# Two-column size sums, a deeper fold of layer 1 scores and staged operand sums in a two-layer attention and SwiGLU kernel

## The chip, the cores and the metric

The kernel runs on one core of one Trainium2 chip. Its time is the device time of one execution in microseconds. A figure for a kernel is the median of several executions; where two kernels are compared, both ran in the same rounds on the same chip.

## The reference, cut to what matters

```python
# x: 1 x 2048 x 1024; all inputs bf16; the same weights in both layers
def A(x, wqkv, wo):      # attention, 32 heads of 32; each position sees 8 keys, 2 apart, backwards
    ...                  # q, k, v = x @ wqkv; softmax over the 8 scores; sum of values; @ wo
def B(x, w1, w3, w2):    # F = 3584
    return (silu(x @ w1) * (x @ w3)) @ w2

for layer in range(2):
    x = x + A(layernorm(x), wqkv, wo)
    x = x + B(layernorm(x), w1, w3, w2)
```

## The kernel before

The positions are cut into four chunks of 512. Eight stages (layer, chunk) of B follow one another on TensorE (PE), with the attention of later chunks woven in. The first two stages of B multiply plainly. While they run, ScalarE and VectorE make scaled fp16 sums and differences of weight blocks and store them; the other six stages use a scheme with seven products of half-size blocks instead of eight, which needs those weights and four sums of the activations.

**The order of instructions on each engine is decided when the program is built, by a model of time inside the kernel.** Every helper adds a modelled cost to a modelled clock, and `background` gives VectorE a waiting piece of work only if it is modelled to fit before the next piece that PE needs. On the chip each engine then goes through its list in that order: the two traces of the kernel after show the same order of all 2126 instructions on VectorE, 1388 on ScalarE and 308 on GpSimd.

```python
def pe(n, ready=0.0):
    now["pe"] = max(now["pe"], ready) + n * MM            # MM = 0.216
    return now["pe"] + 0.1
def dve(cost, ready=0.0):
    now["dve"] = max(now["dve"], ready) + cost
    ...
def dma(kb, ready=0.0, issue=0.45):                       # modelled landing of a load
    now["sp"] = max(now["sp"], ready, now["dma"] - 9.0) + issue
    now["dma"] = max(now["dma"], now["sp"] + 0.2) + kb / 380
    return now["dma"] + 1.3
def background(until):
    while True:
        best = None
        for queue in (norms, makes, adds, values, scores):
            step = head(queue)                            # (cost, ready, emit)
            if step is not None:
                start = max(now["dve"] + 0.3, step[1])
                if start - 0.3 + step[0] <= until and (best is None or start < best[0]):
                    best = start, queue
        if best is None:
            return
        take(best[1])
```

The parts that the change touches (cut):

```python
def norm_sums(key):                       # four sums of activations for a stage of B
    while not sums_free[0]:
        yield "blocked"                   # until the stage before has left all three buffers
    ...
    yield step(s1, a21, a22, ALU.add)         # each: cost 0.62, ready when xnT is modelled to land
    yield step(s2, s1, a11, ALU.subtract)
    yield step(a21, a11, a21, ALU.subtract)
    yield step(s4, a12, s2, ALU.subtract)

def weight_size(m, g, w, at, got):        # squares of a weight group, summed over partitions
    ...
    for i in range(2):
        nc.tensor.matmul(ps[:], lhsT=ones[:], rhs=size[:, m, g, i:i + 1], start=i == 0, stop=i == 1)
    makes.append([scale_item(ps, pe(2, t)), None])

def differences(m, g, a, r):              # VectorE, for stored weight blocks
    for out, x, y in ((4, 5, 1), (1, 1, 0), (2, 5, 1), (6, 3, 2)):
        yield 0.46, r, lambda: nc.vector.tensor_tensor(b[:, out], b[:, x], b[:, y], op=ALU.subtract)

def score_steps():                        # per half chunk
    ...
    yield 0.0, ready + 2.0, lambda: None  # modelled landing of kT, plus 2 us
    yield from tree(W, tree_bufs[0], mul_qk, lambda w_: psm[:, w_], True)   # leaves two partials
    ...
    for i in range(2):                    # gather: sums over a head's dimensions, on PE
        for a in range(4):
            nc.tensor.matmul(L[32 * a:32 * (a + 1), :, :], lhsT=gather[:],
                             rhs=psm[:, :, i, a * BLK:(a + 1) * BLK], start=i == 0, stop=i == 1, ...)
    at["t"] = pe(3, t) + 0.2

def b_stage(u, hold):
    ...
    if u >= TU:
        force(adds, lambda: ("B", l, c) in sums_of)       # all four sums before the first product
```

In the profile these are named by what they write: `L` is the gather, `psm` a partial of the scores, `st` the gate and up products of the fast scheme, `w` the down product, `ps` a projection to q, k or v, `po` the output projection, `xnT` the transposed normed input, and `big` a buffer that holds, among others, weight differences and operand sums.

## Time and profile before

| | before |
|---|---|
| median, lowest to highest (three executions; the result below has a fourth) | 1545.78 us, 1545.72 to 1547.3 |
| PE busy, of a span of 1546.5 us | 1529.9 us (99%) |
| VectorE (DVE) busy | 1191.9 us (77%) |
| PE's waits, all together | 12.5 us |

The profiled execution itself took 1548.26 us, longer than the timed ones. The first lines of the page of the kernel before (PEld is TensorE's loading of weights, ACT is ScalarE, POOL is GpSimd; SPq, further down, is SyncE, which issues loads and stores):

```profile
span 1546.5 us, 25176 instructions
PE 1529.9 (99%) x9694; PEld 992.7 (64%) x9694; DVE 1191.9 (77%) x2048; ACT 883.3 (57%) x1388; POOL 158.8 (10%) x308
```

PE is the bound. A busy PE need not be an efficient one, so the starts of matmuls were looked at as well: they follow each other at 215 to 216 ns with 512 columns and 109 ns with 256 nearly everywhere. What is to be won is PE's own work and its few waits. From the list of what PE waited for (engine, line, tile, releaser: us in total, times, longest):

```profile
PE L L595 <- DVE psm L506: 4.1, 1, 4.1
PE w L1057 <- DVE hT L1028: 2.6, 3, 1.4
PE w L1057 <- ACT big L1077: 1.9, 4, 0.6
```

The largest wait is a single one, and the timeline shows its making (start us, length us, engine, line, operation, in brackets the idle time just before and what ended it):

```profile
522.88 8.33 SPq L831 DMA_DIRECT2D qkv_d<-hT  x2
531.30 8.73 SPq L263 DMA_TRANSPOSE xnT<-xn  x2
...
542.21 0.69 DVE L287 TENSOR_TENSOR big<-xnT 128x1024 f16<-128x1024 f16 x1 [10.08 <-DMA xnT<-xn]
...
545.68 0.42 DVE L506 TENSOR_TENSOR psm<-tree 128x512 bf16<-128x512 bf16 x1
546.16 1.05 PE L595 MATMUL L<-psm,gather 128*32 128x512 bf16 x8 [4.06 <-DVE psm L506]
...
554.49 1.22 DVE L582 TENSOR_TENSOR tree<-qT,kT 128x2048 bf16<-128x2048 bf16 x1 [1.46 <-DMA kT<-qkv_d]
```

SyncE issues two transposed loads only after two stores, which wait for PE's pace. VectorE stands 10 us at the first operand sum (L287), for those loads; the last folds of `psm` stand behind it in the list, though their inputs are there; PE's gather waits for the folds. The Trainium skill ("TensorE: Matmul & The Clock Gate", specification table, engine queue depth) calls VectorE's queue strict FIFO, and this is what it looks like.

The stall has a second cost. The windows view (start and end, length, busy time of the engines, granted PE clock, DMA share, GB/s) shows the clock of the stretch:

```profile
541.00:560.00 19.00, 14.94 (x63) 7.97 (x61) 12.94 (x19) 5.39 (x8) 2.19 (x4) 0.82 1.01 317
```

Eleven matmuls after the stall start 427 ns apart instead of 216, 2.3 us more. The skill (same page, Part 1) says that an idle window of about 3.4 us halves the clock; here an idle of 4.1 us did.

The groups whose counts the change alters or whose cost it moves (line, engine, operation, tiles, shapes, count, then busy us and mean ns of one, then idle before):

```profile
L595 PE MATMUL L<-psm,gather 128*32 128x512 bf16 x128 | 10.3, 399 | 4.1 <-DVE psm L506 4.1
L872 PE MATMUL size<-size,ones 128*128 128x1 f32 x56 | 7.0, 229 | 0.0
```

These durations overlap. What a burst delays PE is read from starts instead: the time from the start of the matmul before it to the start of the one after it, less that matmul's usual 216 or 109 ns. A size burst (two fp32 matmuls, each in two records) costs 0.363 us, with starts 28, 112, 112 and 111 ns apart. In the same way a wait comes out some 0.2 us longer from the starts than the idle time that the views list; where the text gives a longer figure than the view, it is from the starts. A gather burst of eight costs 0.641 us: four start 2 to 5 ns apart, 216 ns later the next four. The skill ("TensorE: Matmul & The Clock Gate", Part 3) gives about 4 ns between matmuls in separate column tiles; the trace agrees.

### The profile page before, as it was taken

What the parts mean: (1) busy time and instruction counts of PE and PEld (TensorE: products, weight loads), DVE (VectorE), ACT (ScalarE), POOL (GpSimd) and SP (SyncE); (2) the same over time, 40 slices, a digit from 0 to 9 for tenths busy, and PEclk for the clock granted to TensorE, in tenths of its full rate; (3) what the DMA queues carried; (4) which work ended last, traced back from release to release, by engine and by line L of the source; (5) the groups of instructions that cost most, each with busy time, mean ns of one, the idle gap of its engine ahead of it and who ended that gap; (6) DMA issues with size and microseconds to landing.
All of it is one profiled execution on the core that took longest, in us unless ns stands there. A gap on an engine that the chain in (4) does not pass through costs nothing.

```text
span 1546.5 us, 25176 instructions
## 1 busy us (share of the span) xinstructions
PE 1529.9 (99%) x9694; PEld 992.7 (64%) x9694; DVE 1191.9 (77%) x2048; ACT 883.3 (57%) x1388; POOL 158.8 (10%) x308
## 2 busy tenths in 40 slices
PE   9999999999999989999999999999999999999999
PEld 7666644444444568675685766866677667686866
DVE  4788988889889688989798958798668977435345
ACT  4885466657565346555574564756557446554633
POOL 1210102111111000101001020100101001000000
PEclk9999999999999999999999999999999999999999
DMA  9777969798898798979979888797979988878885
GB/s 330 202 222 203 265 222 319 255 305 284 249 329 290 241 307 316 316 265 295 296 269 339 309 261 284 277 318 275 334 249 316 339 296 276 303 275 327 311 292 207
DMA packets 261432, 439.57 MB, mean 284 GB/s; under 512 B 73856, under 2 KB 201088, under 8 KB 245056
## 3 DMA queue, kind: packets, MB, share of 16 engines
q1 hardware_dynamic: 248464, 390.90, 76.6%
q0 software_dynamic: 12704, 46.93, 8.2%
q8 instruction: 76, 1.25, 0.3%
q14 instruction: 44, 0.36, 0.1%
q10 hardware_dynamic: 144, 0.13, 0.0%
HBM read 345.90 MB, written 67.90 MB: 268 GB/s over the span
## 4 chain that ended last, share of the span: by engine, by line
PE 83%; DVE 9%; ACT 3%; DMA 3%; issue 1%; POOL 1%; SPq 1%; ACTq 0%; DVEq 0%; POOLq 0%
PE st L1122 28%; PE ps L820 18%; PE w L1057 11%; PE po L762 7%; PE pg L1243 6%; PE acc L1274 6%; PE pu L1252 6%; DVE tree L656 1%; DMA wqkv<-in_A_wqkv_dram 1%; DVE tree L502 1%; PE pq L436 1%; DVE tree L582 1%; DVE hT L1028 1%; DMA xnT<-xn 1%; DVE hT L1140 1%
## 5 line engine op out<-in xcount | busy, mean ns | idle before, releaser
L820 PE MATMUL ps<-xnT,wqkv 128*128 128x512 f16 (+1 forms) x1472 | 323.3, 381 | 0.3 <-DMA wqkv<-in_A_wqkv_dram 0.2
L1122 PEld LDWEIGHTS <-early 128*128 128x128 f16 x2688 | 262.8, 98 | 38.2 <-issue 1.4
L820 PEld LDWEIGHTS <-wqkv 128*128 128x128 bf16 x1472 | 210.7, 144 | 111.8 <-issue 5.8
L1057 PE MATMUL w<-t,hT 128*128 128x512 f16 x1008 | 226.4, 379 | 4.6 <-DVE hT L1028 2.6
L1122 PEld LDWEIGHTS <-late 128*128 128x128 f16 x2016 | 197.0, 98 | 31.2 <-issue 3.2
L582 DVE TENSOR_TENSOR tree<-qT,kT 128x2048 bf16<-128x2048 bf16 x128 | 156.3, 1221 | 30.0 <-ACT big L824 14.8
L502 DVE TENSOR_TENSOR tree<-tree 128x1024 bf16<-128x1024 bf16 x256 | 175.1, 684 | 0.9
L1122 PE MATMUL st<-xnT,late 128*128 128x256 f16 x1344 | 174.2, 273 | 1.0 <-DVE big L1178 0.7
L1057 PEld LDWEIGHTS <-hT 128*128 128x128 f16 x1008 | 98.0, 98 | 118.5 <-DVE hT L1028 5.4
L1122 PE MATMUL st<-big,early 128*128 128x256 f16 x1344 | 172.2, 273 | 0.2
L1122 PE MATMUL st<-xnT,early 128*128 128x256 f16 x1344 | 165.7, 273 | 0.0
L656 DVE TENSOR_TENSOR tree<-At,vT 128x2048 bf16<-128x2048 bf16 x128 | 156.2, 1220 | 7.9 <-DMA At<-E 6.5
L1151 ACT COPY st<-st 128x512 f32<-128x512 f32 x84 | 48.4, 576 | 125.1 <-PE st L1122 124.3
L762 PE MATMUL po<-wo,oT 128*128 128x512 bf16 x512 | 115.9, 379 | 0.9 <-DVE x_sb L767 0.9
L1252 PE MATMUL pu<-xnT,w3t 128*128 128x512 f16 x448 | 105.8, 379 | 0.0
L1243 PE MATMUL pg<-xnT,w1t 128*128 128x512 f16 x448 | 105.8, 379 | 0.0
L824 ACT CAST hT<-ps 128x512 bf16<-128x512 f32 x96 | 55.6, 585 | 81.5 <-PE ps L820 80.3
L1163 DVE TENSOR_TENSOR st<-st,big 128x512 f32<-128x512 f32 x84 | 58.4, 695 | 51.9 <-ACT big L1160 51.8
L1274 PE MATMUL acc<-w2t,hT 128*128 128x512 bf16 x448 | 98.2, 379 | 0.0
L1131 ACT ACTIVATE sg<-st,down_scale 128x512 bf16<-128x512 f32 x126 | 86.5, 687 | 11.5 <-PE st L1122 10.9
L1122 PE MATMUL st<-big,late 128*128 128x256 f16 x672 | 87.1, 273 | 0.0
L762 PEld LDWEIGHTS <-oT 128*128 128x128 bf16 x512 | 50.1, 98 | 56.8 <-issue 1.2
(166 smaller groups left out, 1912.0 us busy)
## 6 DMA issues: line engine op xcount, KB each, us to landing
early<-t_d SPq DMA_DIRECT2D x84, 1024.0 KB, 6.5
late<-t_d SPq DMA_DIRECT2D x84, 768.0 KB, 6.4
t<-t_d SPq DMA_DIRECT2D x42, 1024.0 KB, 7.1
t<-t_d SPq DMA_DIRECT2D x42, 768.0 KB, 5.3
wqkv<-in_A_wqkv_dram SPq DMA_DIRECT2D x28, 1024.0 KB, 8.2
w1t<-in_B_w_dram SPq DMA_DIRECT2D x14, 1024.0 KB, 9.3
w3t<-in_B_w_dram SPq DMA_DIRECT2D x14, 1024.0 KB, 11.5
t_d<-big POOLq DMA_DIRECT2D x28, 512.0 KB, 7.1
```

Of the source, the lines that this page charges most:

```text
L502: nc.vector.tensor_tensor(b, b, buf[:, 4:8, :], op=ALU.add)
L582: V.tensor_tensor(pr, qT[:], kT[:, :, k0:k0 + TCH], op=ALU.mult)
L656: V.tensor_tensor(tm.rearrange("p w (a e) -> p w a e", a=4), At[:].rearrange("p a w e -> p w a e"), win, op=ALU.mult)
L762: nc.tensor.matmul(ps[:], lhsT=oT[:, t, j * P:(j + 1) * P], rhs=wo[:, t, hh * 512:(hh + 1) * 512], start=(t == 0), stop=(t == KT - 1))
L820: nc.tensor.matmul(ps[:], lhsT=ws[kk // KH][:, kk % KH, t::KT], rhs=xnT[:, kk, :], start=(kk == 0), stop=(kk == KT - 1))
L1057: nc.tensor.matmul(out[:], lhsT=lhs[:, k, j * P:(j + 1) * P], rhs=w[:, k, :], start=start and k == 0, stop=k == nq - 1, skip_group_check=True)
L1122: nc.tensor.matmul(out[:, a, :], lhsT=w[:, a, blk, k, :], rhs=rhs[:, k, :], start=start and a == 0 and k == 0, stop=k == KQ - 1, skip_grou ...
L1131: nc.scalar.activation(sg[:], src, ACTF.Silu, scale=inv)
L1163: nc.vector.tensor_tensor(G["D"][:], G["D"][:], su, op=ALU.add)
L1243: nc.tensor.matmul(pg[:], lhsT=w1t[:, kk, fi * P:(fi + 1) * P], rhs=xnT[:, kk, :], start=(kk == 0), stop=(kk == KT - 1))
L1252: nc.tensor.matmul(pu[:], lhsT=w3t[:, kk, fi * P:(fi + 1) * P], rhs=xnT[:, kk, :], start=(kk == 0), stop=(kk == KT - 1))
L1274: nc.tensor.matmul(acc[:], lhsT=hT[:, f, j * P:(j + 1) * P], rhs=tiles[hh][f // nq][:, f % nq, :], start=(f == 0), stop=(f == f1 - f0 - 1))
```

## The change

Its intent: take small matmuls off PE, hand scales and operand sums out as early as their inputs and buffers allow, and make VectorE's weight differences less serial. The diff also adds three functions that would use the fast scheme for the v projection (`size_of_v`, `sums_of_v`, `v_products`), and moves the product pipeline into a function of its own for them. They are never called. The core, cut:

```diff
 def norm_sums(key):
-    while not sums_free[0]:
-        yield "blocked"
-    sums_free[0] = False
     ...
-    yield step(s1, a21, a22, ALU.add)
-    yield step(s2, s1, a11, ALU.subtract)
-    yield step(a21, a11, a21, ALU.subtract)
-    yield step(s4, a12, s2, ALU.subtract)
+    for name, i, out, x, y, op in (("P5", 0, s1, a21, a22, ALU.add), ("P6", 1, s2, s1, a11, ALU.subtract),
+                                   ("P3", 2, s4, a12, s2, ALU.subtract), ("P7", 3, a21, a11, a21, ALU.subtract)):
+        while (sums_free[i] is None) if i < 3 else key in plain_left:
+            yield "blocked"
+        ...
+        yield 0.61, ready, lambda: nc.vector.tensor_tensor(out, x, y, op=op)
+        sums_at[key, name] = now["dve"] + 0.1
     # a buffer is free after the last product that reads it; run() forces only the sum it needs
@@ score_steps
-    yield from tree(W, tree_bufs[0], mul_qk, lambda w_: psm[:, w_], True)
+    parts_ = 2 if l == 0 else 1
+    yield from tree(W, tree_bufs[0], mul_qk, lambda w_: psm[:, w_, 0:parts_], l == 0)
     ...
-        for i in range(2):
+        for i in range(parts_):
-        at["t"] = pe(3, t) + 0.2
+        at["t"] = pe(1.5 * parts_, t) + 0.2
@@ weight_size
-                scale_of(ps[:], up, down)
+                nc.vector.tensor_reduce(down, ps[:], op=ALU.add, axis=AX.X)
+                scale_of(down, up, down)
-            for i in range(2):
-                nc.tensor.matmul(ps[:], lhsT=ones[:], rhs=size[:, m, g, i:i + 1], start=i == 0, stop=i == 1)
-            makes.append([scale_item(ps, pe(2, t)), None])
+            nc.tensor.matmul(ps[:], lhsT=ones[:], rhs=size[:, m, g, :], start=True, stop=True)
+            makes.insert(0, [scale_item(ps, pe(1, t)), None])
@@ differences (and the same for the down weights)
-        for out, x, y in ((4, 5, 1), (1, 1, 0), (2, 5, 1), (6, 3, 2)):
-            yield 0.46, r, lambda: nc.vector.tensor_tensor(b[:, out], b[:, x], b[:, y], op=ALU.subtract)
+        for out, x, y in ((4, 5, 1), (1, 1, 0), (2, 4, 0), (6, 3, 2)):
+            yield 0.40, r, lambda: nc.vector.tensor_tensor(
+                b[:, out], b[:, x], b[:, y], op=ALU.add if (x, y) == (4, 0) else ALU.subtract)
@@ not shown: side_tile() takes open scales before it hands out a side buffer; a scale's modelled cost goes from 0.8 to 1.0; the unused v functions
```

## The prediction

> **What bounds the kernel now.** TensorE. The page shows PE busy 99% of 1546.5 us at a granted clock of 0.997; VectorE 77%, ScalarE 57%. Matmuls start one after another at 216 ns (512 columns) and 109 ns (256) nearly everywhere. The list of waits gives PE only 12.5 us in all. The largest, 4.1 us, is at 546.2: the head-gathering matmul of scores (L) waits for VectorE's psm. The timeline shows why: VectorE stands 10.1 us at 542.2 at the first operand sum, for a transposed load of xnT that was queued behind two stores on SyncE. After it eleven matmuls take about 427 instead of 216 ns (granted clock 0.82 in 541 to 560, windows view), so the place costs some 6.5 us. The Trainium skill ("TensorE: Matmul & The Clock Gate", Part 1) says that an idle window of about 3.4 us halves the clock; the trace agrees. Other PE waits: 2.6 us for hT sums and 1.9 us for copies in the down product, 0.9 us each for the rest.
>
> **What the change does.** The three new functions for V (sizes, sums, products) are never called: 0 us.
> 1. Size of a weight group: four fp32 passes x14 become two. A burst now delays PE by 0.363 us; its starts are 28, 112, 112, 111 ns apart, so about 0.22 us goes: 14 x 0.22 = 3.1 us of PE. VectorE gains a tiny reduce (0.17 us, as the existing one) x14 = 2.4 us. Scales go to the front of their queue.
> 2. Layer 1 scores: a gather burst goes from 8 to 4 matmuls; it costs 0.641 us, its second half 0.216 us: 8 x 0.216 = 1.7 us of PE. VectorE gets 64 more folds like oT<-tree, 0.285 us each: 18 us over layer 1, where it is busy 601 of 723 us (windows).
> 3. Differences: the third no longer reads the second's result; some 0.06 to 0.1 us x42, 3 to 4 us of VectorE.
> 4. Operand sums staged per buffer, forced only before the product that needs them: PE waits for them today only through the stall at 546, and there the transposes are late, not the buffers. Nothing directly.
>
> **On the critical path.** 1 and 2 come off PE, the bound: -4.8 us. 3, 4 and the added folds are off it, but shift the kernel's modelled clocks, which decide the order of instructions; small waits may go or appear. Whether the stall stays depends on whether the transposes are issued before or after a store; I give 40% that it goes (-2.6 us in the mean), and +1 to 2 us for new waits on a busier VectorE. Together about 1540 us, 0.4% faster; 8 in 10 between 1533 and 1547.
>
> Chances: faster by over 2% 0.01, within 2% 0.97, slower by over 2% 0.02.
>
> **What would show it.** Size matmuls 56 to 28, bursts delaying PE 0.14 us; gather matmuls 128 to 96, layer 1 bursts 0.43 us; folds of 128x256 from 128 to 192; VectorE busy up by 10 to 16 us, PE busy down by 5; PE's waits with or without the 4.1 us on psm, and that stretch's clock.
>
> **What would make it wrong.** A reordering that puts VectorE behind a late load elsewhere (4 us plus a cold clock each); the added folds delaying the sums before the down product; scales forced early stalling VectorE; the stall moving rather than going.

## The result

| | before | after |
|---|---|---|
| first measurement, median (lowest to highest) | 1546.04 us (1545.72 to 1547.3) | 1544.22 us (1543.84 to 1544.88) |
| ratio, 95% interval | | 0.9987 (0.997 to 1.0004) |
| second measurement, five rounds, median | 1547.29 us | 1543.54 us |
| ratio, 95% interval | | 0.9975 (0.9963 to 0.9988) |
| span of the profiled execution | 1546.5 us | 1542.1 us |

A ratio is the mean time of one kernel's runs over that of the other's of the same rounds, so it is not quite the ratio of the medians. With five rounds the gain is clear of noise, at 2 to 6 us. The two traces differ by 4.4 us, more than the medians do (1.8 and 3.8 us): the trace of the kernel before is of an execution that was slower than its timed ones.

The page of the kernel after:

```profile
span 1542.1 us, 25098 instructions
PE 1521.5 (99%) x9595; PEld 990.2 (64%) x9634; DVE 1200.9 (78%) x2126; ACT 884.8 (57%) x1388; POOL 156.8 (10%) x308
```

The counts show that some matmul records are missing: 9634 weight loads, but 9595 matmuls. So "PE busy" is not to be compared to the microsecond here, and the starts of matmuls that both traces have are used. The altered groups, after:

```profile
L609 PE MATMUL L<-psm,gather 128*32 128x512 bf16 x96 | 8.1, 386 | 0.9 <-DVE psm L519 0.9
L897 PE MATMUL size<-size,ones 128*128 128x2 f32 x28 | 3.9, 209 | 0.0
...
L519 DVE TENSOR_TENSOR psm<-tree 128x256 bf16<-128x256 bf16 x64 | 18.3, 285 | 0.3
```

Size records went from 56 to 28 and a burst from 0.363 to 0.140 us. Layer 1 has four gathers in a burst, which costs 0.426 us instead of 0.641. VectorE has the 64 new folds, 18.3 us when their durations are added; its busy time rose by 9.0 us, a little less than the 10 to 16 of the prediction. PE's waits are another list than before, and together they went from 12.5 to 14.5 us:

```profile
PE st L1086 <- DVE st L1110: 3.8, 1, 3.8
PE ps L841 <- ACT hT L845: 1.8, 1, 1.8
PE po L776 <- DVE x_sb L781: 1.6, 2, 0.8
PE st L1086 <- DVE big L303: 1.4, 1, 1.4
...
PE ps L841 <- DMA wqkv<-in_A_wqkv_dram: 1.2, 2, 1.0
PE L L609 <- DVE psm L519: 0.9, 1, 0.9
```

The wait of 4.1 us on `psm` is gone; one of 3.8 us on a sum of `st` has come, and others in the projection `ps`, in `po` and, at 941 us, for an operand sum (`big`). The waits of `w` for `hT` (2.6 us) are gone too. The timeline of the stretch in which the stall stood:

```profile
526.91 4.48 PE L841 MATMUL ps<-xnT,wqkv 128*128 128x512 f16 x20 [1.81 <-ACT hT L845]
...
528.99 0.68 DVE L303 TENSOR_TENSOR big<-xnT 128x1024 f16<-128x1024 f16 x1
...
532.36 11.45 PE L841 MATMUL ps<-xnT,wqkv 128*128 128x512 f16 x52 [0.97 <-DMA wqkv<-in_A_wqkv_dram]
...
554.50 1.23 DVE L595 TENSOR_TENSOR tree<-qT,kT 128x2048 bf16<-128x2048 bf16 x1 [4.29 <-DMA kT<-qkv_d]
...
568.61 0.68 DVE L515 TENSOR_TENSOR tree<-tree 128x1024 bf16<-128x1024 bf16 x1
569.22 0.69 DVE L1110 TENSOR_TENSOR st<-st,big 128x512 f32<-128x512 f32 x1
...
569.96 1.87 PE L1086 MATMUL st<-big,late 128*128 128x256 f16 x8 [3.80 <-DVE st L1110]
```

The operand sum now finds its loads landed (no idle before 528.99), so PE reaches the stage of `st` sooner: at 559.9 instead of 566.8. But `kT` is used from 554.5 on, as before to the hundredth. VectorE has the folds of those scores, and products of values, in its list ahead of the sum of `st` (L1110) that PE needs, so PE waits for it. The stall did not go; it moved by 24 us. The clock follows it (windows view, after):

```profile
541.00:560.00 19.00, 19.00 (x96) 12.15 (x94) 9.10 (x12) 7.53 (x12) 2.20 (x4) 1.00 1.04 339
...
570.00:574.00 4.00, 4.00 (x25) 3.08 (x25) 4.00 (x7) 2.33 (x4) 0.00 (x0) 0.65 0.43 177
```

How the lead of the kernel after grows and shrinks is best seen from the starts of the same matmul (counted within its kind) in both traces:

```
start before   start after   difference   what lies since the row above
   192.0          192.6         +0.6      start of the program, loads
   487.5          484.0         -3.5      14 shorter size bursts; a wait of 1.1 us for po at 216 gone
   537.6          537.6          0.0      new waits of PE at 515, 532 (for loads) and 527 (for ScalarE)
   557.8          550.8         -6.9      the stall on psm and its cold clock gone
   577.8          576.2         -1.6      the new stall at 570 and its cold clock
   924.0          923.9         -0.1      new waits of 0.9 to 1.1 us at 612, 756 and 759; shorter gathers
  1126.6         1123.7         -2.9      waits of w for hT gone, shorter gathers; a new wait of 1.6 us at 941
  1267.1         1263.3         -3.8      one wait of 0.8 us of w gone, shorter gathers
  1546.5         1542.1         -4.4      a second wait of 0.8 us of w gone
```

### The profile page after: what moved, and what is told of

The parts are those of the page before. It is cut to its first block, busy times and chain, and to the rows that moved or that the text cites. A ratio compares the mean times of both kernels' runs of the same rounds, so it can differ in the third digit from the quotient of the medians. Undisturbed runs are those within 1.5% of the kernel's fastest.

```text
span 1542.1 us, 25098 instructions
## 1 busy us (share of the span) xinstructions
PE 1521.5 (99%) x9595; PEld 990.2 (64%) x9634; DVE 1200.9 (78%) x2126; ACT 884.8 (57%) x1388; POOL 156.8 (10%) x308
## 4 chain that ended last, share of the span: by engine, by line
PE 55%; DVE 4%; DMA 3%; ACT 3%; issue 1%; POOL 1%; ACTq 0%; DVEq 0%; POOLq 0%
PE st L1086 29%; PE w L1235 15%; PE ps L841 6%; PE po L776 4%; DMA qkv_d<-hT 1%; DMA t_d<-big 1%; DMA kT<-qkv_d 1%; DVE tree L595 1%; DMA xnT<-xn 1%; DVE tree L515 1%; ACT sg L1297 0%; DVE tree L670 0%; ACT big L1043 0%; ACT xn L323 0%; ACT L1297 0%
## 5 line engine op out<-in xcount | busy, mean ns | idle before, releaser
L776 PE MATMUL po<-wo,oT 128*128 128x512 bf16 x487 | 111.6, 379 | 2.9 <-DVE x_sb L781 1.6
L1110 DVE TENSOR_TENSOR st<-st,big 128x512 f32<-128x512 f32 x84 | 58.4, 695 | 50.2 <-ACT big L1107 50.1
```

What stands on the lines that cost most here:

```text
L776: nc.tensor.matmul(ps[:], lhsT=oT[:, t, j * P:(j + 1) * P], rhs=wo[:, t, hh * 512:(hh + 1) * 512], start=(t == 0), stop=(t == KT - 1))
L1110: nc.vector.tensor_tensor(G["D"][:], G["D"][:], su, op=ALU.add)
```

## The experiments

Twelve kernels were run, each with five rounds against the kernel before, and all gave a correct result. The theory with which they started was A: PE's saved work is saved time, and the rest is the order that the model makes of it. Its rivals are in the expectations.

### The size part alone

```diff
 # the kernel before, with the reduce and the two-column matmul of the change; still append, pe(2, t), cost 0.8
```

The order of all other instructions was compared with that of the kernel before and is the same; only the 14 reduces are new on VectorE.

> The kernel before with the two-column size matmul and the small reduce alone; the modelled costs are left as they were, so that every other instruction stands where it stood. Theory A (PE work saved is time saved): 14 bursts lose 0.22 us each, so about 3.1 us faster, ratio 0.998; the 4.1 us stall on psm near 543 stays, as does its cold clock. Theory B (what the change saved was never on the critical path, the 1.8 us came from a different order): within 0.5 us of the kernel before.

Measured: 1545.17 us against 1547.29, ratio 0.9987 (0.9975 to 1.0). In the traces the size bursts lose 3.1 us in all, each visible as a step of 0.22 us, and the end comes 2.2 us sooner; waits that are 0.4 to 0.8 us longer than before, among them one for a wqkv load at 1085 us, take the rest. The stall stays (3.9 us at 545). Theory A holds for this part, at two thirds of its size.

### The fold alone, in the old order

```diff
 # the kernel before; layer 1: four gathers, and after each psm of two partials one more add
+    V.tensor_tensor(psm[:, w_, 0:1], psm[:, w_, 0:1], psm[:, w_, 1:2], op=ALU.add)
 # no modelled cost for it, and the gather still counted as pe(3, t)
```

> The kernel before with the extra fold of layer 1 scores and the halved gather alone, modelled costs kept, so the order is that of before with 64 folds put in. Theory A: 8 bursts lose 0.216 us each, 1.7 us faster, ratio 0.9989, and VectorE's 18 us more cost nothing. Theory C (the folds are paid for by PE in layer 1): waits of the down product for VectorE's sums grow from 2.6 us and the kernel is as fast as before or up to 3 us slower.

Measured: 1549.03 us against 1547.29, ratio 1.0012 (0.9999 to 1.0024): slower, if anything. Eight steps of 0.22 us are there in the starts, and more is lost between 880 and 1090 us. PE's waits in 850 to 1110 us were 2.6, 0.7, 0.4 and 0.2 us before; with the fold they are

```profile
PE w L1065 <- DVE hT L1036: 2.6, 3, 1.5
PE st L1130 <- ACT st L1159: 0.9, 1, 0.9
...
```

and six more lines of 0.3 to 0.7 us. Theory C is the right one here, in another shape than it was put: the wait for `hT` did not grow, new ones came. VectorE's 18 us were not free.

### Both parts, in the old order

> Both parts in the order of the kernel before. Theory A: the savings add, 4.8 us faster, about 1541.2 us, which is faster than the whole change (1544.2); then the order of the whole change costs some 3 us. Theory B or C: no faster than the whole change.

Measured: 1547.74 us against 1547.29, ratio 1.0007 (0.9994 to 1.0021); the trace ends 1.1 us sooner than that of before. The parts do not bring 4.8 us: the fold eats what the size part gives.

### The whole change, again

> The whole change once more on the same chip as the three parts, for a narrow interval: 1.8 us faster than before if the medians so far hold, 4.4 us if the two traces do. Theory A with a dearer order: slower than the two parts alone by 2 to 4 us.

Measured: 1543.54 us, ratio 0.9975 (0.9963 to 0.9988). So the whole is better than its two PE savings in the old order, against what theory A expected: the new order does not cost 3 us, it is worth some.

### The fold as the change writes it

```diff
 # the kernel before, with the tree and the gather of the change, their costs in the model
-            yield from tree(W, tree_bufs[0], mul_qk, lambda w_: psm[:, w_], True)
+            parts_ = 2 if l == 0 else 1
+            yield from tree(W, tree_bufs[0], mul_qk, lambda w_: psm[:, w_, 0:parts_], l == 0)
```

> The kernel before with the fold of layer 1 scores as the change writes it: the folds and the shorter gather stand in the kernel's own model of time, so the order may move. Theory D (the 1.7 us that the fold cost in the old order came from VectorE running later than its model says, at three places between 985 and 1090 us): with the folds in the model the gathers' 1.7 us are kept, ratio 0.998 to 0.999. Rival (VectorE is simply too busy there and the fold costs whatever the model knows): ratio 1.001 as in the fold alone.

Measured: 1544.59 us against 1547.38, ratio 0.9981 (0.9968 to 0.9993). The same folds and gathers as in the fold alone: there about 1.7 us slower than before, here 2.8 us faster. Of PE's waits in 850 to 1110 us there are left:

```profile
PE st L1123 <- ACT big L1161: 2.2, 1, 2.2
PE w L1058 <- ACT big L1078: 0.5, 1, 0.5
```

The waits of `w` for `hT` are gone. That the folds are in the model is the only difference in the text of the two programs that matters; what it did is another order (some 200 of 2112 VectorE instructions stand elsewhere than in the kernel before), and how much of the 4.5 us is foresight and how much luck, this pair cannot tell.

### The size part with that fold

```diff
 # the kernel before with the fold as in the kernel above, and the size part as in the first experiment; nothing else
```

Apart from the size sums and their reduces, all engines have the order of the kernel above.

> The kernel before with the size part and the fold as the change writes it, nothing else: no staging, no new differences, no new queue places. If the parts add: 2.1 + 2.8 = 4.9 us faster, ratio 0.9968, a little faster than the whole change (0.9975 in its round). If they don't: like the fold alone, 0.998.

Measured: 1541.99 us (1541.46 to 1543.66) against 1546.93, ratio 0.9969 (0.9955 to 0.9983), and a trace of 1540.0 us. In this order the parts add: 2.1 us for the size part and 2.8 for the fold, measured apart, make 4.9, and 4.9 is what both bring. Two of the change's parts are thus worth about as much as the whole (0.9975, 0.9963 to 0.9988; the intervals overlap), although the old stall is still there:

```profile
PE L L596 <- DVE psm L506: 3.9, 1, 3.9
```

### The whole change without its fold

> The whole change without its fold (layer 1 keeps two partials and eight gathers). Theory D: slower than the whole change by about 1.7 us (ratio to before 0.9985 against 0.9975). Rival: faster than the whole change by 1 to 2 us (0.9965). The late part has another order either way, so up to 1.5 us of it may be that.

Measured: 1543.53 us against 1547.38, ratio 0.9971 (0.9958 to 0.9983), and a trace 0.1 us shorter than that of the whole change. Theory D, which had it slower, is not met. The rival's 0.9965 lies inside the interval, but the two traces are of one length: within the change, the fold is worth nothing that can be measured. What it takes off PE, 1.7 us, comes back as waits in the late part; the trace without it has no wait of PE at 941 us and none before the gather at 756 (1.6 and 1.1 us with it), and from 578 to 1538 us it gains 1.5 us on the whole change.

### The whole change without staging

```diff
-            while (sums_free[i] is None) if i < 3 else key in plain_left:
-                yield "blocked"
+        while not all_free[0]:
+            yield "blocked"          # and: order P5, P6, P7, P3; all forced at the start of the stage
```

> The whole change with the operand sums as before (all four at once when all three buffers are free, forced at the start of the stage). The two programs differ in the order of 29 of 2128 VectorE instructions. My reading (PE never waits for a buffer of sums): within 0.5 us of the whole change, ratio 0.9975. Rival (staging is what the change is for): slower by 2 us or more, with new PE waits at the start of the stages.

Measured: 1545.47 us against 1547.38, ratio 0.999 (0.9976 to 1.0004), where the whole change had 0.9975 in its rounds. The intervals overlap, so the traces decide. Without staging PE waits at 1262.9 and at 1405.4 us, 0.8 us each, as in the kernel before at 1266.0 and 1408.5; with it these waits are gone. In the kernel before, the four sums for the next stage stand in one piece in front of a sum that the down product needs:

```profile
1262.06 0.68 DVE L287 TENSOR_TENSOR big<-xnT 128x1024 f16<-128x1024 f16 x1
...
1263.99 0.68 DVE L287 TENSOR_TENSOR big<-xnT,big 128x1024 f16<-128x1024 f16 x1
1264.60 0.69 DVE L1080 TENSOR_TENSOR w<-w,big 128x512 f32<-128x512 f32 x1
1265.38 0.59 ACT L1077 COPY big<-w 128x512 f32<-128x512 f32 x1 [1.95 <-DVE w L1080]
...
1266.01 3.18 PE L1057 MATMUL w<-t,hT 128*128 128x512 f16 x14 [0.62 <-ACT big L1077]
```

In the kernel after they are spread over the products before, as each buffer comes free:

```profile
1244.79 0.68 DVE L303 TENSOR_TENSOR big<-xnT 128x1024 f16<-128x1024 f16 x1
...
1252.71 0.69 DVE L303 TENSOR_TENSOR xnT<-xnT 128x1024 f16<-128x1024 f16 x1
...
1258.19 9.12 PE L1235 MATMUL w<-t,hT 128*128 128x512 f16 x41
...
1260.77 0.69 DVE L1258 TENSOR_TENSOR w<-w,big 128x512 f32<-128x512 f32 x1
```

Staging pays, then, at the two places where one fast stage follows another directly: between the starts of the same matmuls the traces with and without it part there by 0.7 and by 0.6 us, 1.3 us together. It does so not because PE waited for a sum, but because four sums in a row made something else late. The trace without staging also has a wait of 1.9 us near 302 us, of `po` on `x_sb`, at a place where the two programs have the same instructions in the same order; in the second trace of the whole change it is 0.5 us long in the starts. It is variation between runs, and it is made up, mostly because the stall at 570 is here followed by no cold clock; at 1200 us the two traces are level.

### The size part, operand sums later

```diff
 # the size part alone, and for the stage whose loads came late:
-            return 0.62, xnT_at[key], lambda: ...
+            return 0.62, xnT_at[key] + (9.0 if key == ("B", 0, 2) else 0.0), lambda: ...
```

> The size part alone, with the operand sums of the first gate/up stage of the fast scheme modelled as ready 9 us later, so that VectorE folds psm before it stands waiting for the transposes. The stall of 3.9 us at 545 and its 1.9 us of cold clock go. Theory E (the stall is moved, not removed: the load of kT for the next half lands at about 554 either way and PE meets VectorE's backlog near 570, as in the whole change): a new PE wait of 3 to 5 us near 570 and under 2 us of gain over the size part. Rival (the stall stands alone): 5 to 6 us faster than the size part, ratio to before 0.995.

Measured: 1550.93 us against 1547.38, ratio 1.0024 (1.0012 to 1.0037): slower than before, and 5 to 6 us slower than the size part alone. The stall at 545 is gone as meant. Its place is taken by

```profile
PE st L1122 <- DVE st L1163: 6.0, 1, 6.0
...
PE st L1122 <- DVE big L287: 2.2, 1, 2.2
```

at 570 (with 21 cold matmuls, 2.2 us) and 941 us. Against the start of the same matmul in the size part alone the lead is 7.3 us at 562 and a lag of 1.2 at 577. Theory E, that the stall moves, is confirmed, and the loss is larger than it was put.

### The differences alone

```diff
 # the kernel before with differences() and the sums of the down weights as in the change
-            yield 0.46, r, ... (2, 5, 1) ... subtract
+            yield 0.40, r, ... (2, 4, 0) ... add
```

> The kernel before with the new differences alone, as the change writes them: the third reads the first's result, and all are counted as 0.40 instead of 0.46 us. No work on PE changes. By the model's own clocks the transposes of the stage at 560 us are then issued 18 us sooner. Theory E: the stall of 4 us on psm goes and one of 3 to 6 us near 570 comes, with 1 to 3 us near 527 to 533: 1544 to 1548 us, ratio 0.998 to 1.001. Rival (the shorter dependence itself is the gain): no stall anywhere in 520 to 575 and 5 us or more faster, 0.9965.

Measured: 1553.16 us against 1546.93, ratio 1.0035 (1.0022 to 1.0047): the part that was to make VectorE lighter makes the kernel slower, and slower than either expectation had it. VectorE's busy time did fall, from 1191.9 to 1188.7 us. It has the waits of the whole change at 527 to 539 and at 577 us, without its savings:

```profile
PE st L1124 <- DVE st L1165: 4.4, 1, 4.4
...
PE ps L820 <- ACT hT L824: 2.1, 1, 2.1
...
PE ps L820 <- DMA wqkv<-in_A_wqkv_dram: 1.7, 2, 1.3
```

So the differences suffice to move the stall. That they do it through the modelled cost and not through being shorter was not tested by a run of its own; it follows from the order, which is fixed when the program is built and knows the modelled costs alone: the model's own clock puts the last two norms of the stage at 510 us instead of 527.5, and so their transposed loads in front of the stores instead of behind them. The other parts shift the same place too; with the two-column size sums at the change's modelled costs (`pe(1, t)`, and 1.0 for a scale) the model puts it at 545 us, and with the scales at the front of their queue as well, as the change has them, at 529 us (read from built programs, not run).

### The whole change, scores of one half later

If theory E is right, one number cures it: in the model `kT` of the second half of the last layer 0 chunk is ready at 545.4 us, where the stage of `st` begins at 556.7. In the trace they are at 554.5 and 559.9, so against the stage the model has the load some 6 us too early.

```diff
-            yield 0.0, ready + 2.0, lambda: None
+            yield 0.0, ready + (8.0 if (l, h) == (0, 7) else 2.0), lambda: None
```

> The whole change, with one number in the kernel's model altered: the scores of the second half of the last layer 0 chunk are counted as ready 8 us, not 2 us, after their modelled load, because in the trace kT landed some 6 us later than the model had it. Theory E (PE's 3.9 us near 570 come from folds put ahead of the sum that PE needs): that wait and its 1.5 us of cold clock go, 4 to 5.4 us faster than the whole change, about 1538.5 us, ratio to before 0.994. Rival (the stretch is bound by its loads and the time comes back as another wait): within 1.5 us of the whole change, ratio 0.997.

Measured: 1534.69 us (1534.23 to 1535.42, four runs) against 1546.93, ratio 0.9919 (0.9906 to 0.9933). PE's waits:

```profile
PE ps L841 <- ACT hT L845: 2.0, 1, 2.0
...
PE st L1086 <- DVE big L303: 1.1, 1, 1.1
PE ps L841 <- DMA wqkv<-in_A_wqkv_dram: 1.0, 1, 1.0
```

The wait near 570 and its cold clock are gone, 5.3 us between the starts of the same matmuls of the two traces, as expected. 3 us more than expected came from behind it: the waits of `po` for `x_sb` at 612 and 759 us, 0.9 us each, and one of 1.1 us for the gather at 756 are gone as well. None of the three is in the kernel before. They went with the new order; that they are its consequence is argued and was not tested.

### And differences before norms

```diff
 # on top of the version above
-        for queue in (norms, makes, adds, values, scores):
+        for queue in (makes, norms, adds, values, scores):
```

> The version with the later scores, and VectorE's choice between equal starts turned: differences and scales go before norms. In the trace of the whole change the last two blocks of differences stand behind norms at 499 and 505 us, so ScalarE's sums of the down weights and with them the release of weight tiles come late, and PE waits 2.0 us at 527 (for ScalarE) and 1.2 us at 532 (for a wqkv load). Theory F (that is their cause): both waits go, about 3 us faster than the later scores alone, 1531.5 us, ratio 0.990, if the transposes, now behind the differences, do not become late. Rival (the stretch 520 to 570 us is full of loads and stores): the waits stay or come back as one for the transposes of 2 to 4 us, ratio 0.991 to 0.994.

Measured: 1534.26 us against 1547.2, ratio 0.992 (0.9907 to 0.9934), the same as without. The two waits went from 3.4 us to 0.7 and the kernel leads the version above by 3.6 us at 544 us, so theory F names their cause rightly. The gain that it promised did not come: the ratio lies in the range of the rival, though not with the wait for the transposes that the rival named. The lead is gone again by the end:

```profile
PE st L1086 <- ACT big L1107: 2.2, 1, 2.2
PE st L1086 <- ACT sg L1297: 1.4, 1, 1.4
```

These are at 991 and 601 us, far from the edit. The best version is one of these two, 12 to 13 us faster than the kernel before and 8 to 9 faster than the change; between them the measurements do not choose.

## Why the prediction was right or wrong

The time was right: 1540 us were predicted, in a range of 1533 to 1547, and 1544.2 and 1543.5 were measured. The range held no gain at all as well; of the 6 us forecast, 1.8 and 3.8 came. The sum behind it was not right in each term, and that its errors partly cancelled was luck.

1. **Size bursts, "about 0.22 us goes: 14 x 0.22 = 3.1 us of PE": right.** A burst went from 0.363 to 0.140 us; 3.1 us in the trace, about 2 us in time when done alone.
2. **Gathers, "8 x 0.216 = 1.7 us of PE", with the added folds "off" the critical path: the first half right, the second wrong.** The burst costs 0.426 us as said (0.43). But the 18.3 us of folds are not free on a VectorE that was busy 601 of 723 us: put into the old order they cost PE more than the gathers give (+1.7 us), and in the whole change the fold is worth nothing. A busy share of 83% was read as room. What counts is whether VectorE is in time at the few places where PE waits for it.
3. **Differences, "some 0.06 to 0.1 us x42, 3 to 4 us of VectorE": right in size, wrong in effect.** Four now take 1.68 us instead of 1.79, and alone they took 3.3 us off VectorE's busy time. The prediction had them only "shift the kernel's modelled clocks". They do, and alone this costs 5 to 6 us.
4. **Staging, "Nothing directly": wrong by some 1.3 us.** The prediction asked whether PE waits for a sum. It should have asked what stands behind the sums in VectorE's list.
5. **The stall, "I give 40% that it goes (-2.6 us in the mean)": it went, and the mean was the wrong thing to reckon with.** The term counted its going as a gain of 6.5 us. It was 6.9 us between the starts of the same matmuls, and 8.8 us came back within some 60 us of time: 3.5 before it (515, 527 and 532) and 5.3 behind it (570). "The stall moving rather than going" stood among the things that would make the prediction wrong; it is what happened, and the term in the sum should have been near zero. The line that showed it was in the trace of before: `kT` landing at 554.5, the next thing that VectorE waits for.

The named terms of the traces' difference: -3.1 (size), -1.7 (gathers), -6.9 (old stall), +3.5 and +5.3 (new ones), -1.3 (staging), together -4.2, beside -4.4 between the traces. That this comes so near is in part luck. Left out are new waits of 0.9 to 1.1 us at 612, 756 and 759 and of 1.6 at 941, and against them the gone waits of `w` for `hT` (2.6 us in the waits list) and of `po` at 216 (1.1).

What stays open: how much of the waits at 612, 756 and 759 us, and of their going, the change of order explains; and how much of the layer 1 gain of a fold that the model knows is foresight and how much is a lucky order.

## What to carry to other kernels

When an in-order engine stands at a late load, everything behind it is late; before counting its removal as a gain, find the next load or backlog that the freed engine will meet, and reckon to that. In a kernel whose order comes from modelled times, a change of cost is a change of order everywhere: try a part with the old order kept, and correct the model where the trace contradicts it; here one corrected landing time was worth more than the whole change. A saving on the bound engine that is paid for on another one is worth only what is left when that one is in time for its consumers, however low its busy share.

## What the Trainium skill lacked or had wrong

- "TensorE: Matmul & The Clock Gate", Back-to-back issue gap: it gives about 131 ns (512 columns) and 81 ns (128) as sustained spacing in streams of weight load and matmul. In such streams this kernel has 215 to 216 ns and 55 to 56 ns, what the page calls the isolated gap.
- The same page, Part 1: for a stall inside a kernel it lacks how widely the cost varies near its 3.4 us window. In the six kernels that kept the stall before the gather, an idle of 3.8 to 4.6 us was followed by 5 to 11 matmuls at half speed (1.0 to 2.3 us more), the longest idle by the fewest. At the stall near 570, one of 3.8 us was followed by twelve of 256 columns (1.25 us), one of 3.4 us (the whole change without its fold) by fourteen (1.4 us), and one of 3.5 us (without staging) by none.
- "FP8 and Floating Point Precision", TensorE Precision Notes: true fp32 is said to take four passes. The trace records each fp32 matmul as two weight loads of 190 ns with two matmuls, which start 28 or 112 ns apart; one on a 128x128 operand with two columns delays PE by 0.140 us. No page has this cost.
- No page says that an instruction's place in a strict FIFO queue can cost more than its work: four sums of 0.69 us, placed in one piece, delayed PE by 0.8 us twice.
